# A fused attention and gated-MLP kernel: the order of VectorE's queue behind the projection, smaller pieces of the p v products, and the eviction of the first chunk

## The chip, the cores and the metric

The kernel runs on one core of a Trainium2 chip. The metric is the device time of one execution in microseconds (us). All runs told of here were with a granted TensorE clock of 1.00. Times are medians. The span of a profile (first to last instruction) is 1.7 to 1.8 us shorter than the device time of the same run. The four engines are TensorE (PE; its weight loads are PEld), VectorE (DVE), ScalarE (ACT) and GpSimd (POOL); SyncE (SP) issues the DMAs.

## The reference

Two residual blocks over x (2048 tokens, width 1024, bf16):

```python
h  = x + A(layernorm(x))       # attention, 32 heads of 32, four segments of 512 tokens;
                               # a memory M, z of phi(k) v is carried from segment to segment
h2 = h + B(layernorm(h))       # gated MLP: gelu(x @ w_in) in halves z1, z2; z2 is normalized,
                               # mixed over tokens by w_sp; (z1 * g) @ w_out
# in A, for each head and segment:
p   = softmax(q k^T * scale + mask)
o   = g * (phi(q) M) / (phi(q) z + 1e-6) + (1 - g) * (p v)
phi = lambda t: where(t > 0, t + 1, exp(t))     # the "feature map"
M, z = M + phi(k)^T v, z + sum(phi(k))
```

## The kernel before

A recording layer notes every operation in program order, and each engine executes its own in exactly that order. A wait is inserted only where the layer sees a dependency: in PSUM per bank, in SBUF per cell of 32 bytes (`GRAN`).

```python
GRAN = 32
# ...
MZB = cb("mzb", [128, NQ, 4, 34], BF16)      # 4*34*2 = 272 bytes for each of NQ = 8 groups of heads
# ...
def next_bank():                             # from n = 0 on, rot["banks"] = [6, 7]
    b = rot["banks"][rot["n"] % len(rot["banks"])]
    rot["n"] += 1
    return b

def pe_T(dst, tcl, src):                     # a 128 x 1024 chunk is transposed by TensorE, evicted by ScalarE
    b = next_bank()
    bb = bank(b).bitcast(BF16)
    for i in range(8):
        pe.transpose(bb[:, i * 128:(i + 1) * 128], src[:, i * 128:(i + 1) * 128], IDENT[:])
    act.activation(dst[:, :, tcl * 128:(tcl + 1) * 128], bb.rearrange("p (c n) -> p c n", c=8), ACTF.Copy)

def phi(n):
    # ...
    act.activation(e, q, ACTF.Exp)
    dve.tensor_single_scalar(p, q, 1.0, ALU.add)      # profile: pqk<-qk
    dve.tensor_single_scalar(e, e, 1.0, ALU.min)      # profile: etmp<-etmp
    dve.tensor_tensor(p, p, e, ALU.max)               # profile: pqk<-pqk,etmp
    # ... DMA transpose of the k half

def wo(s, tcl, half):                                 # output projection and residual
    # ...
    b = next_bank()
    mm8(bank(b), ...)                                 # profile: ps<-wo,oT
    dve.tensor_tensor(HCH[tc % 3][:, hs], XR[tc % 2][:, hs], bank(b), ALU.add)   # profile: hch<-xr,ps
    # ...

# the main loop, one round for each group of four heads and each segment
for n in range(LAST + 1):
    # ... f1, f2: K and Q products of round n + 1; f3, f4: V products or halves of wo
    split = bool(s > 0 and c > 0 and not f4)
    logits(n, 0)                              # scores, banks 0 to 3, then exp (e_104 or e_107)
    fill(f1)
    if n > 0:
        pv(n - 1, (0, 1) if split else (0, 1, 2, 3))
    logits(n, 1)                              # exp: e_105 or e_108
    if n > 0:
        state(n - 1)                          # writes msum and mzb
    bg_pop()                                  # pieces of layer norms, from a queue
    fill(f2)
    logits(n, 2)                              # exp: e_106 or e_109; mem (reads mzb), then tm by VectorE
    # ...
    if n < LAST:
        phi(n + 1)
    fill(f3)
    if split:
        pv(n - 1, (2, 3))
    bg_pop()
    fill(f4)
    bg_pop()
    # ...
```

A round asks five times for one of two banks (f1, state, f2, f3, f4). So f1 of a round takes the bank of the preceding round's f3, and f3 takes the bank that `state` used.

The softmax here doesn't subtract the row's maximum and nothing guards it: scores larger than these inputs give would overflow.

Of the kernel before, what the change touches and what calls it, by code (L numbers as in the profile page):

```python
# [5 lines left out]
BF16 = mybir.dt.bfloat16  # L6
F32 = mybir.dt.float32
I32 = mybir.dt.int32
ACTF = mybir.ActivationFunctionType
# [5 lines left out]
NSEG = 4  # L15
# [4 lines left out]
NQ = 8  # L20
# [237 lines left out]
def bass_sequential_preLN__memory_aug_infini_attn__mixer_gmlp__prompt_kernel(  # L258
# [17 lines left out]
    pe, act, dve, pool, sp = R.pe, R.act, R.dve, R.pool, R.sp  # L276
# [6 lines left out]
    def tens(name, shape, dt, off):  # L283
        sz = int(np.prod(shape[1:])) * mybir.dt.size(dt)
        assert off % 32 == 0 and off + sz <= ARENA, (name, off, sz)
        t = nc.alloc_sbuf_tensor_at(name, list(shape), dt, offset=abase + off)
        R.space[t[:].tensor.name] = ("sbuf", off)
        return t
# [14 lines left out]
    IDENT = cb("ident", [128, 128], BF16)  # L303
# [19 lines left out]
    XNT = [tens("xnT0", [128, 8, L], BF16, 30 * K), tens("xnT1", [128, 8, L], BF16, 38 * K)]  # L323
# [10 lines left out]
    XCH = [b2("xch%d" % i, [128, D], BF16) for i in range(4)]  # L334
    QK = [b2("qk%d" % i, [128, 2, L], BF16) for i in range(2)]
    PQK = [b2("pqk%d" % i, [128, 2, L], BF16) for i in range(2)]
    ETMP = b2("etmp", [128, 2, L], BF16)
# [25 lines left out]
    def bank(b):  # L363
        return PS[:, b, :]
# [6 lines left out]
    def next_bank():  # L371
# [4 lines that stand above are left out]
    def mm8(dst, lhs, rhs, n=8):  # L376
        for i in range(n):
            pe.matmul(dst, lhs(i), rhs(i), start=(i == 0), stop=(i == n - 1))
# [61 lines left out]
    def ln_apply(src, k):  # L440
        o = LNO[lno[0] % 3]
        lno[0] += 1
        dve.tensor_scalar(o[:], src[:], MV[k][:, 0:1], RS[k][:, 1:2], ALU.subtract, ALU.mult)
        return o
# [1 line left out]
    def to_T(dst, tcl, src):  # L446
        sp.dma_start_transpose(dst[:, :, tcl * 128:(tcl + 1) * 128], src[:])

    def pe_T(dst, tcl, src):
        b = next_bank()  # L450
        bb = bank(b).bitcast(BF16)
        for i in range(8):
            pe.transpose(bb[:, i * 128:(i + 1) * 128], src[:, i * 128:(i + 1) * 128], IDENT[:])
        act.activation(dst[:, :, tcl * 128:(tcl + 1) * 128], bb.rearrange("p (c n) -> p c n", c=8), ACTF.Copy)


    def proj_v(s, tcl, half):
# [2 lines left out]
    def proj_v_cols(s, tcl, lo, w):  # L460
        b = next_bank()
        xt = XNT[s % 2]
        mm8(PS[:, b, 0:w], lambda i: xt[:, i, tcl * 128:(tcl + 1) * 128], lambda i: WV[:, i, lo:lo + w])
        act.activation(V[:, tcl, lo // 32:(lo + w) // 32, 0:32],
                       PS[:, b, 0:w].rearrange("p (h d) -> p h d", d=32), ACTF.Copy)
# [6 lines left out]
        mm8(bank(b), lambda i: w[:, i, c * 128:(c + 1) * 128], lambda i: xt[:, i, :])  # L472
        act.activation(QK[n % 2][:, which, :], bank(b), ACTF.Copy)

    def phi(n):
        s, c = divmod(n, NQ)
        lo = 1 if s == 0 else 0
        hi = 1 if s == NSEG - 1 else 2
        q, p, e = QK[n % 2][:, lo:hi, :], PQK[n % 2][:, lo:hi, :], ETMP[:, lo:hi, :]
        act.activation(e, q, ACTF.Exp)  # L480
        dve.tensor_single_scalar(p, q, 1.0, ALU.add)
        dve.tensor_single_scalar(e, e, 1.0, ALU.min)
        dve.tensor_tensor(p, p, e, ALU.max)
        if s < NSEG - 1:
            sp.dma_start_transpose(PK[n % 3][:], PQK[n % 2][:, 1, :])


    def logits(n, rnd):
        qk = QK[n % 2]
        parts = {0: ((0, 0, 512),), 1: ((1, 0, 384), (3, 384, 128)), 2: ((2, 0, 256),)}[rnd]  # L490
        wid = (512, 512, 256)[rnd]
        e = E[n % 2][rnd]
        for j, o, w in parts:
            for i in range(4):
                pe.matmul(PS[:, i, o:o + w], qk[32 * i:32 * (i + 1), 1, j * 128:(j + 1) * 128],
                          qk[32 * i:32 * (i + 1), 0, j * 128:512], start=True, stop=True,
                          tile_position=(32 * i, 0))
        if rnd == 2 and n >= NQ:
            mem(n)
        act.activation(e[:, :, 0:wid], PS[:, 0:4, 0:wid], ACTF.Exp, scale=float(SCALE))  # L500
        for j, o, w in parts:
            d = e[:, :, o:o + 128]
            pool.affine_select(out=d, in_=d, pattern=[[0, 4], [1, 128]], compare_op=ALU.is_ge, fill=0.0,
                               base=0, channel_multiplier=-1)
        if rnd == 2 and n >= NQ:
            mem_norm(n)

    def pv(n, cqs):
        c = n % NQ
        for cq in cqs:  # L510
            for j in range(cq + 1):
                rnd, o = {0: (0, cq * 128), 1: (1, cq * 128 - 128), 2: (2, cq * 128 - 256), 3: (1, 384)}[j]
                for i in range(4):
                    pe.matmul(PVA[:, cq, i, :], E[n % 2][rnd][:, i, o:o + 128], V[:, j, 4 * c + i, 0:33],
                              start=(cq % 2 == 0 and j == 0 and i == 0), stop=False, skip_group_check=True)
        if 3 in cqs:
            norm(n)
# [61 lines left out]
    def ln_tasks(src, dst, tcl):  # L579
        lnq[0].append((src, dst, tcl))  # L580
# [14 lines left out]
    ks = {}  # L595

    def stats_of(tc):
        ks[tc] = ln_stats(XCH[tc])
        ln_rstd(ks[tc])


    def warm(k):
        for _ in range(k):
            pe.matmul(bank(7), IDENT[:], ETMP[:, 0, :], start=True, stop=True)

    warm(12)
    stats_of(0)
    stats_of(1)
    late = {1: [(0, 0), (0, 1)], 2: [(1, 0), (1, 1)], 3: [(2, 0), (2, 1), (3, 0), (3, 1)]}

    lns = [ln_apply(XCH[0], ks[0]), ln_apply(XCH[1], ks[1])]
    for tc in range(4):
        if tc < 2:
            stats_of(tc + 2)
        pe_T(XNT[0], tc, lns[tc])
        if tc < 2:
            warm(3)
        if tc in (1, 2):
            lns.append(ln_apply(XCH[tc + 1], ks[tc + 1]))
        for t_, q in late.get(tc, []):  # L620
            proj_v_cols(0, t_, 256 * q, 256)
    for tc in range(4, 8):
        x_load(tc)
    sp.dma_start(WK[:, :, 256:D], wcols(A_wk, 256, D))
# [1 line left out]
    gates()  # L626
    proj_qk(0, 1)
    proj_qk(0, 0)
    phi(0)
    rot["banks"] = [6, 7]  # L630

    CH = [("z2", FH + 448 * k, 448) for k in range(4)] + [("z1", 512 * k, min(512, FH - 512 * k)) for k in range(4)]
# [29 lines left out]
    LAST = NSEG * NQ - 1  # L662
    for n in range(LAST + 1):
        s, c = divmod(n, NQ)
        f1, f2, f3, f4 = [], [], [], []
        if n < LAST:
            f1, f2 = [("qk", n + 1, 1)], [("qk", n + 1, 0)]
        if s == 0:
            f3 = [("v", 0, c, 1)] if c < 4 else [("v", 1, c - 4, 0)]
        elif s < NSEG - 1:  # L670
            if c < 2:
                f3, f4 = [("v", s, 2 * c, 1)], [("v", s, 2 * c + 1, 1)]
            elif c < 6:
                f3, f4 = [("wo", s - 1, c - 2, 0)], [("wo", s - 1, c - 2, 1)]
            else:
                f3, f4 = [("v", s + 1, 2 * (c - 6), 0)], [("v", s + 1, 2 * (c - 6) + 1, 0)]
        else:
            if c < 4:
                f3 = [("v", s, c, 1)]
            if c in (2, 3):  # L680
                f4 = [("wo", s - 1, 0, c - 2)]
            elif c in (4, 5):
                f3 = [("wo", s - 1, 1, c - 4)]
            elif c == 6:
                f3, f4 = [("wo", s - 1, 2, 0)], [("wo", s - 1, 2, 1)]
            elif c == 7:
                f1, f2 = [("wo", s - 1, 3, 0)], [("wo", s - 1, 3, 1)]
                f3, f4 = [("z2", 0, 0)], [("z2", 0, 1)]

        def fill(lst):  # L690
            for u in lst:
                {"v": proj_v, "wo": wo, "qk": proj_qk, "z2": z2_group}[u[0]](*u[1:])

        if s < NSEG - 1 and c < 4:
            ln_tasks(XCH[c], XNT[(s + 1) % 2], c)
        if s < NSEG - 2 and c >= 4:
            x_load(4 * (s + 2) + c - 4)
        if s > 0 and c == 1:
            xr_load(4 * (s - 1))

        split = bool(s > 0 and c > 0 and not f4)
        logits(n, 0)
# [3 lines that stand above are left out]
        logits(n, 1)  # L706
        if n > 0:
            state(n - 1)
        bg_pop()
        fill(f2)  # L710
        logits(n, 2)
        if n == 0:
            mask_g()
        if n < LAST:
            phi(n + 1)
        fill(f3)
        if split:
            pv(n - 1, (2, 3))
        bg_pop()
        fill(f4)  # L720
        bg_pop()
        if n == 1:
            sp.dma_start(WO[:], wcols(A_wo, 0, D))
        if n in (28, 29):
            win_load(n - 28)
# [31 lines left out]
    for k in range(4, 8):  # L757
        lo, w = CH[k][1:]
        for fl in range(w // 128):
            fc = lo // 128 + fl  # L760
            for s in range(NSEG):
                b = next_bank()
# [11 lines left out]
    for tb in range(4):  # L774
# [4 lines left out]
        for fc in range(14):  # L779
            b = next_bank()  # L780
# [3 lines left out]
        for tcl in range(4):  # L784
            tc = 4 * tb + tcl
            fin = FIN[tc % 3]
            sp.dma_start(fin[:], out2d[tc * 128:(tc + 1) * 128, :])
            for lo, w in ((0, 512), (512, 512)) if tc < NTC - 1 else ((0, 512), (512, 256), (768, 256)):
                b = next_bank()
# [34 lines left out]
```

## Time and profile before

| | |
|---|---|
| time | 811.35 us (811.25 to 811.51) |
| TensorE busy, clock | 98%, 1.00 |
| a full round, from its first score product to the next round's | 9.57 us |
| the eight "late" rounds, each directly behind a projection (four from 111.21, four from 190.24 us) | 10.19 us |
| the three split rounds (from 249.08, 275.99 and 283.81 us) | 7.81, 7.82, 8.32 us |

The prediction calls the late rounds "projection rounds". The projection's products are at the end of one round and the wait for their bank is at the head of the following one; a late round is counted from the score product just ahead of that wait.

From the page of the kernel before: its span, the engines' busy times with their shares of the span and instruction counts, and one of the costliest groups (busy us, mean ns of one, then the idle time ahead of it):

```profile
span 809.5 us, 12478 instructions
...
PE 791.0 (98%) x5335; PEld 384.3 (47%) x5408; DVE 369.3 (46%) x755; ACT 302.7 (37%) x356; POOL 121.1 (15%) x234
...
L209 PE MATMUL ps<-wo,oT 128*128 128x512 bf16 x252 | 57.8, 379 | 0.3 <-DVE rd L209 0.2
```

A matmul of 512 columns takes 379 ns by its record, and there is hardly any idle time ahead of such groups. Only the stages in which TensorE waits can give something back. From the list of TensorE's waits (who waited for whom: us in total, times, longest):

```profile
PE ps L209 <- DVE hch_85 L209: 1.7, 3, 0.6
PE ps L209 <- DVE hch_86 L209: 1.6, 3, 0.6
PE ps L209 <- DVE hch_87 L209: 1.1, 2, 0.6
...
PE ps L209 <- ACT qk_96 L209: 0.7, 1, 0.7
...
PE ps L209 <- ACT e_105 L209: 0.6, 4, 0.2
PE ps L209 <- ACT e_108 L209: 0.6, 4, 0.2
```

The three hch lines are one kind of wait in three rotating buffers: 8 waits, 4.4 us. The timeline (start, us, engine, operation, in brackets the idle time ahead of it and what ended it) shows one of them:

```profile
119.61 0.69 DVE L209 TENSOR_TENSOR tm_112<-ps,rdm 128x512 f32<-128x512 f32 x1
120.22 0.42 DVE L209 TENSOR_SCALAR pqk_98<-qk_96 128x1024 bf16<-128x1024 bf16 x1
120.55 0.42 DVE L209 TENSOR_SCALAR etmp<-etmp 128x1024 bf16<-128x1024 bf16 x1
121.00 0.69 DVE L209 TENSOR_TENSOR pqk_98<-pqk_98,etmp 128x1024 bf16<-128x1024 bf16 x1
121.40 0.39 PE L209 MATMUL ps<-qk_96 32*128 32x512 bf16 x4
121.61 0.68 DVE L209 TENSOR_TENSOR hch_86<-xr_84,ps 128x512 bf16<-128x512 bf16 x1
...
122.35 1.90 PE L209 MATMUL ps<-xnT_78,wk 128*128 128x512 bf16 x8 [0.55 <-DVE hch_86 L209]
```

VectorE runs the three operations of the feature map (120.22 to 121.61) between tm and the residual addition hch. TensorE's K product needs the bank that hch empties. The feature map itself is not needed until a round later. The late round is longer than a full one by 10.19 - 9.57 = 0.62 us; the bracket says 0.55, since ends of matmuls are modelled.

One of the split rounds, at the place where the next round begins:

```profile
280.83 0.29 PE L209 MATMUL ps<-qk_96 32*128 32x256 bf16 x4 [0.15 <-ACT e_105 L209]
...
283.05 0.69 DVE L209 TENSOR_TENSOR tm_111<-ps,rdm 128x512 f32<-128x512 f32 x1
...
283.81 0.40 PE L209 MATMUL ps<-qk_97 32*128 32x512 bf16 x4
```

No wait is reported at 283.81, yet tm ends at 283.74, and the product may not start before tm has read its banks. There is no slack behind the visible absence of a wait.

The start of the kernel:

```profile
6.62 0.49 DVE L209 TENSOR_SCALAR lno_88<-xch_92,mv_63,rs_67 128x1024 bf16<-128x1024 bf16 x1
...
7.89 0.55 DVE L209 TENSOR_SCALAR lno_89<-xch_93,mv_64,rs_68 128x1024 bf16<-128x1024 bf16 x1 [0.77 <-POOL rs_68 L209]
...
21.80 0.60 ACT L209 ACTIVATE qk_96<-ps 128x512 bf16<-128x512 f32 x1 [1.13 <-PE ps L209]
...
22.45 0.39 PE L209 MATMUL ps<-qk_96 32*128 32x512 bf16 x4 [0.69 <-ACT qk_96 L209]
...
22.90 1.88 ACT L209 ACTIVATE e_104<-ps 128x2048 bf16<-128x2048 f32 x1
```

lno_88 and lno_89 are the first two normalized chunks of x. The statistics and normalizations are in one VectorE queue (GpSimd makes rs between them), and TensorE's transposes wait for them.

### The profile page before, as it was taken

How to read it: one execution, taken by the hardware profiler on the slowest of the kernel's cores; microseconds unless marked ns; L12 is line 12 of the kernel's file. 1: busy time of each engine (PE TensorE's matmuls, PEld its weight loads, DVE VectorE, ACT ScalarE, POOL GpSimd, SP SyncE). 2: the span in 40 equal slices, each digit the busy share in tenths (PEclk: the TensorE clock that was granted, in tenths of full speed). 3: DMA queues.
4: the chain of work that ended last, by engine and by line, in shares of the span. 5: the costliest groups of instructions: out<-in, count | busy, mean ns of one | idle time of the engine just before them, and what ended most of it. 6: DMA issues, size and time to landing. Idle time of an engine off the chain costs nothing.

```text
span 809.5 us, 12478 instructions
## 1 busy us (share of the span) xinstructions
PE 791.0 (98%) x5335; PEld 384.3 (47%) x5408; DVE 369.3 (46%) x755; ACT 302.7 (37%) x356; POOL 121.1 (15%) x234
## 2 busy tenths in 40 slices
PE   8999999999999999999999999999999999999998
PEld 5445544454454445455554444444444444444444
DVE  4653687668754485844463000054233324423332
ACT  4898866787678764133333333200000000000000
POOL 2343333233323331100131000000000000000000
PEclk9999999999999999999999999999999999999999
DMA  9682535355434055711114100460270044011002
GB/s 291 160 169 60 92 66 131 79 92 72 103 51 79 28 144 124 183 46 53 53 52 106 25 1 0 157 149 0 79 137 1 26 95 94 1 58 53 1 7 85
DMA packets 125992, 64.79 MB, mean 80 GB/s; under 512 B 94832, under 2 KB 114928, under 8 KB 125936
## 3 DMA queue, kind: packets, MB, share of 16 engines
q1 hardware_dynamic: 125936, 63.99, 34.4%
q8 instruction: 42, 0.69, 0.3%
q14 instruction: 14, 0.11, 0.0%
HBM read 32.51 MB, written 8.39 MB: 51 GB/s over the span
## 4 chain that ended last, share of the span: by engine, by line
PE 88%; DVE 6%; ACT 4%; issue 1%; DMA 0%; POOL 0%; DVEq 0%
PE ps L209 88%; ACT e_108 L209 1%; ACT e_105 L209 1%; DVE rdm L209 1%; DVE ta L209 1%; DVE tm_111 L209 1%; DVE stats_59 L209 0%; ACT e_106 L209 0%; DVE stats_61 L209 0%; DVE tm_112 L209 0%; DVE hch_85 L209 0%; DVE etmp L209 0%; ACT e_109 L209 0%; DMA xch_92<-in_A_x_dram 0%; DVE rd L209 0%
## 5 line engine op out<-in xcount | busy, mean ns | idle before, releaser
L209 PE MATMUL ps<-w_out,yT 128*128 128x512 bf16 (+1 forms) x453 | 96.9, 372 | 0.5
L209 PE MATMUL ps<-wspT_122,z_119 128*128 128x512 bf16 x439 | 96.5, 379 | 0.5
L209 PE MATMUL ps<-wspT_121,z_119 128*128 128x512 bf16 x439 | 96.5, 379 | 0.5
L209 PEld LDWEIGHTS ps<-w_out,yT 128*128 128x128 bf16 x462 | 45.2, 98 | 51.7
L209 PEld LDWEIGHTS ps<-wspT_121,z_119 128*128 128x128 bf16 x448 | 43.8, 98 | 52.8
L209 PEld LDWEIGHTS ps<-wspT_122,z_119 128*128 128x128 bf16 x448 | 43.8, 98 | 52.9
L209 DVE TENSOR_TENSOR tmpg_128<-ps,brow_126 128x512 f32<-128x512 f32 x14 | 9.7, 691 | 116.9 <-DMA brow_126<-in_B_b_sp_dram 96.6
L209 ACT ACTIVATE z_119<-ps 128x448 bf16<-128x448 f32 x64 | 34.8, 544 | 75.1 <-PE ps L209 74.9
L209 PE MATMUL ps<-wo,oT 128*128 128x512 bf16 x252 | 57.8, 379 | 0.3 <-DVE rd L209 0.2
L209 ACT ACTIVATE z1T<-ps 128x512 bf16<-128x512 f32 x56 | 33.4, 597 | 63.3 <-PE ps L209 63.3
L209 DVE BATCH_NORM_STATS2 zst<-z_119 128x6 f32<-128x448 bf16 x64 | 39.2, 620 | 33.2 <-ACT z_119 L209 33.2
L209 PEld LDWEIGHTS ps<-wo,oT 128*128 128x128 bf16 x256 | 24.4, 98 | 27.5 <-DVE hch_86 L209 0.3
L209 ACT ACTIVATE e_107<-ps 128x2048 bf16<-128x2048 f32 x16 | 30.0, 1874 | 12.7 <-PE ps L209 12.7
L209 ACT ACTIVATE e_108<-ps 128x2048 bf16<-128x2048 f32 x16 | 30.0, 1878 | 10.8 <-PE ps L209 10.8
L209 ACT ACTIVATE e_104<-ps 128x2048 bf16<-128x2048 f32 x16 | 30.0, 1876 | 10.4 <-PE ps L209 10.4
L209 ACT ACTIVATE e_105<-ps 128x2048 bf16<-128x2048 f32 x16 | 30.0, 1877 | 9.8 <-PE ps L209 9.8
L209 PE MATMUL ps<-xnT_78,wk 128*128 128x512 bf16 x126 | 29.9, 380 | 2.5 <-DVE hch_85 L209 1.1
L209 PE MATMUL ps<-xnT_77,wk 128*128 128x512 bf16 x127 | 30.2, 380 | 2.3 <-DVE hch_86 L209 1.1
L209 PE MATMUL ps<-wv,xnT_78 128*128 128x512 bf16 x128 | 29.6, 379 | 0.0
L209 PE MATMUL ps<-wv,xnT_77 128*128 128x512 bf16 (+1 forms) x159 | 29.5, 336 | 0.1
L209 PE MATMUL ps<-xnT_78,wq 128*128 128x512 bf16 x113 | 27.0, 379 | 1.3 <-issue 0.6
L209 PE MATMUL ps<-xnT_77,wq 128*128 128x512 bf16 x114 | 27.2, 379 | 0.7
(217 smaller groups left out, 1169.6 us busy)
## 6 DMA issues: line engine op xcount, KB each, us to landing
w_out<-in_B_w_out_dram SPq DMA_DIRECT2D x1, 3584.0 KB, 12.7
wo<-in_A_wo_dram SPq DMA_DIRECT2D x1, 2048.0 KB, 10.6
xr_83<-in_A_x_dram SPq DMA_DIRECT2D x8, 256.0 KB, 3.1
xr_84<-in_A_x_dram SPq DMA_DIRECT2D x8, 256.0 KB, 3.0
win_116<-in_B_w_in_dram SPq DMA_DIRECT2D x2, 896.0 KB, 4.9
wk<-in_A_wk_dram SPq DMA_DIRECT2D x1, 1536.0 KB, 11.4
wq<-in_A_wq_dram SPq DMA_DIRECT2D x1, 1536.0 KB, 15.0
out_dram<-hch_85 SPq DMA_DIRECT2D x6, 256.0 KB, 3.0
```

The source lines that it names most:

```text
L209: ins = getattr(e, op.name)(*op.args, **op.kw)
```

## The change

The intent is to take waits out of TensorE's queue. The change has three independent parts. Part 1 moves VectorE's share of the feature map behind f3, so the residual addition goes ahead of it. Part 2 moves the products of p with v (`pv`) for the third token quarter, in the split rounds (those in which f4 is empty), ahead of the third score product. Part 3 evicts the first chunk by ScalarE and VectorE from two banks, and reorders the first V, K and Q products (normalized x with a weight) so that the last V products fill the wait for qk_96.

```diff
-    def pe_T(dst, tcl, src):
-        b = next_bank()
-        ...
+    def pe_T(dst, tcl, src, engines=(act,)):
+        w = 8 // len(engines)
+        for k, eng in enumerate(engines):
+            bb = bank(next_bank()).bitcast(BF16)[:, 0:w * 128]
+            ...                                   # w transposes
+            if eng is act:
+                act.activation(d, v, ACTF.Copy)
+            else:
+                dve.tensor_copy(d, v)
@@
-    def phi(n):
+    def phi_exp(n):
+        q, p, e = phi_views(n)
         act.activation(e, q, ACTF.Exp)
+
+    def phi_max(n):
+        q, p, e = phi_views(n)
         dve.tensor_single_scalar(p, q, 1.0, ALU.add)
         dve.tensor_single_scalar(e, e, 1.0, ALU.min)
         dve.tensor_tensor(p, p, e, ALU.max)
         ...
@@ start: order of the first products
-    # T0 warm(3) | T1 warm(3) V0 | T2 V1 | T3 V2 V3 | K Q | phi(0)
+    # T0 (act, dve) warm(3) | T1 warm(2) V0 | T2 V1 | T3 V2 | K Q V3 | phi_exp(0) phi_max(0)
     ...
@@ main loop
         fill(f2)
+        if split:
+            pv(n - 1, (2,))
         logits(n, 2)
         ...
         if n < LAST:
-            phi(n + 1)
+            phi_exp(n + 1)
         fill(f3)
+        if n < LAST:
+            phi_max(n + 1)
         if split:
-            pv(n - 1, (2, 3))
+            pv(n - 1, (3,))
```

(The start is shown as two comment lines: T is a chunk's transposes, V its two quarter V products; warm(k) is k products whose results nobody reads.)

More of the change, by code (lines that the diff above doesn't have):

```diff
@@ L447, in to_T @@
         sp.dma_start_transpose(dst[:, :, tcl * 128:(tcl + 1) * 128], src[:])
-    def pe_T(dst, tcl, src):
-        b = next_bank()
-        bb = bank(b).bitcast(BF16)
-        for i in range(8):
-            pe.transpose(bb[:, i * 128:(i + 1) * 128], src[:, i * 128:(i + 1) * 128], IDENT[:])
-        act.activation(dst[:, :, tcl * 128:(tcl + 1) * 128], bb.rearrange("p (c n) -> p c n", c=8), ACTF.Copy)
+    def pe_T(dst, tcl, src, engines=(act,)):
+        w = 8 // len(engines)
+        for k, eng in enumerate(engines):
+            bb = bank(next_bank()).bitcast(BF16)[:, 0:w * 128]
+            for i in range(w):
+                o = (k * w + i) * 128
+                pe.transpose(bb[:, i * 128:(i + 1) * 128], src[:, o:o + 128], IDENT[:])
+            d = dst[:, k * w:(k + 1) * w, tcl * 128:(tcl + 1) * 128]
+            v = bb.rearrange("p (c n) -> p c n", c=w)
+            if eng is act:
+                act.activation(d, v, ACTF.Copy)
+            else:
+                dve.tensor_copy(d, v)
     def proj_v(s, tcl, half):
@@ L473, in proj_qk, with phi_views @@
         act.activation(QK[n % 2][:, which, :], bank(b), ACTF.Copy)
-    def phi(n):
-        s, c = divmod(n, NQ)
+    def phi_views(n):
+        s = n // NQ
         lo = 1 if s == 0 else 0
         hi = 1 if s == NSEG - 1 else 2
-        q, p, e = QK[n % 2][:, lo:hi, :], PQK[n % 2][:, lo:hi, :], ETMP[:, lo:hi, :]
+        return QK[n % 2][:, lo:hi, :], PQK[n % 2][:, lo:hi, :], ETMP[:, lo:hi, :]
+    def phi_exp(n):
+        q, p, e = phi_views(n)
         act.activation(e, q, ACTF.Exp)
+    def phi_max(n):
+        q, p, e = phi_views(n)
         dve.tensor_single_scalar(p, q, 1.0, ALU.add)
@@ L483, in phi @@
         dve.tensor_tensor(p, p, e, ALU.max)
-        if s < NSEG - 1:
+        if n // NQ < NSEG - 1:
             sp.dma_start_transpose(PK[n % 3][:], PQK[n % 2][:, 1, :])
@@ L604, in warm, with v_quarter @@
             pe.matmul(bank(7), IDENT[:], ETMP[:, 0, :], start=True, stop=True)
+    def v_quarter(tcl, q):
+        proj_v_cols(0, tcl, 256 * q, 256)
     warm(12)
@@ L608, in bass_sequential_preLN__memory_aug_infini_attn__mixer_gmlp__prompt_kernel @@
     stats_of(1)
-    late = {1: [(0, 0), (0, 1)], 2: [(1, 0), (1, 1)], 3: [(2, 0), (2, 1), (3, 0), (3, 1)]}
-    lns = [ln_apply(XCH[0], ks[0]), ln_apply(XCH[1], ks[1])]
-    for tc in range(4):
-        if tc < 2:
-            stats_of(tc + 2)
-        pe_T(XNT[0], tc, lns[tc])
-        if tc < 2:
-            warm(3)
-        if tc in (1, 2):
-            lns.append(ln_apply(XCH[tc + 1], ks[tc + 1]))
-        for t_, q in late.get(tc, []):
-            proj_v_cols(0, t_, 256 * q, 256)
+    ln0 = ln_apply(XCH[0], ks[0])
+    pe_T(XNT[0], 0, ln0, (act, dve))
+    warm(3)
+    ln1 = ln_apply(XCH[1], ks[1])
+    stats_of(2)
+    pe_T(XNT[0], 1, ln1)
+    warm(2)
+    stats_of(3)
+    v_quarter(0, 0)
+    v_quarter(0, 1)
+    ln2 = ln_apply(XCH[2], ks[2])
+    ln3 = ln_apply(XCH[3], ks[3])
+    pe_T(XNT[0], 2, ln2)
+    v_quarter(1, 0)
+    v_quarter(1, 1)
+    pe_T(XNT[0], 3, ln3)
+    v_quarter(2, 0)
+    v_quarter(2, 1)
     for tc in range(4, 8):
@@ L628, in bass_sequential_preLN__memory_aug_infini_attn__mixer_gmlp__prompt_kernel @@
     proj_qk(0, 0)
-    phi(0)
+    v_quarter(3, 0)
+    v_quarter(3, 1)
+    phi_exp(0)
+    phi_max(0)
     rot["banks"] = [6, 7]
```

## The prediction

> **What bounds the kernel now.** TensorE: the page gives it 791.0 of 809.5 us busy (98%), clock 1.00. The chain of waits is TensorE alone from 329 us on. TensorE's timeline gives the round period: 9.57 us in a full round, but 10.19 us in the eight that compute the output projection (four from 111.2, four from 190.2 us). In each of these TensorE idles 0.55 us before the next K product, released by "hch", VectorE's residual addition that empties the bank (list of waits: 8 waits, 4.4 us). The chain shows tm, then pqk, etmp, pqk (the feature map, about 1.35 us), then hch (0.69 us).
>
> **Part 1, residual ahead of the feature map.** hch can start when tm ends (120.3 us in the round from 111.2) and end near 121.0; TensorE needs the bank about 121.75. The wait should vanish. Gross: 8 x 0.62 = 5.0 us. Deduction: with two layer norms in flight VectorE has about 9.8 us of work in the second such round of each group (0.36 us idle in 10.19), more than 9.57. Its lag should reach "msum" a round later, which frees that projection's bank: I expect a new 0.3 us wait in the third projection round of each group, then slack (VectorE idles 1.56 us there). Net 4.4 us. The round at 292 us: perhaps 0.1.
>
> **Part 2, V products in three parts.** Only three rounds split (from 249, 276 and 284 us). The moved part, 12 products, about 0.30 us, fits the 0.3 us in which TensorE waits for e_105/e_108. But the next round's first product needs e_106/e_109 and then tm, which ends 0.07 us before that product starts already (283.74, 283.81; 292.05, 292.13; 256.82, 256.89). The freed 0.3 us becomes a wait for tm. Worth 0 (-0.1 to +0.2).
>
> **Part 3, first chunk by two engines.** ScalarE's 1.02 us eviction is halved, but TensorE's next transposes wait for lno_89, not for it, and VectorE's new copy stands ahead of lno_89. Estimate: a 512-element PSUM operation takes 0.69 us at one element a cycle; the Trainium skill ("VectorE: DVE Perf Modes", "Why PSUM operands drop a tier") caps a PSUM source at 2x_1P, so about 0.42 us for bf16; no run shows this copy yet. It delays lno_89 (7.89) by 0.3 to 0.5 us, and the chain to lno_90 (11.46) slides along. In return the last V products fill the 0.69 us in which TensorE waited for qk_96, but what follows is a ScalarE chain (qk_96, etmp, e_104): its exp now waits for a 0.38 us V eviction instead of a 0.60 us one. Net: e_104 (22.90 now) starts 0.05 to 0.3 us later; about 0.15 us lost.
>
> **Sum.** 811.35 - 4.4 - 0.1 + 0.15 = 807.0 us, range 806.0 to 808.3. Faster by over 2% 1%, within 98%, slower 1%.
>
> **What would show each step.** Right: no TensorE waits on hch in projection rounds; period 9.6 us, one per group near 9.9 with a wait on msum; from 250 to 300 us unchanged periods (7.81, 7.82, 8.32) and waits on tm in place of e_105/e_108; lno_89 at 8.2 to 8.4, e_104 at 23.0 to 23.2. Wrong: hch waits that only shrink; split rounds 0.2 us shorter; e_104 before 22.8.
>
> **What would make it wrong.** No msum wait (806.5); VectorE's lag reaching tm or hch too (808); a residual load, whose order against the transposes changes, landing late; a copy over 0.7 us; part 2 gaining 0.3 us a round (806).

## The result and the profile after

| | before | after |
|---|---|---|
| time, median | 811.36 us (6 runs) | 806.94 us (6 runs, 806.82 to 807.40) |
| ratio | | 0.9946, 95% interval 0.9933 to 0.9959 |
| late rounds, first group | 10.19, 10.19, 10.19, 10.19 | 9.70, 9.57, 9.68, 9.57 |
| late rounds, second group | 10.18, 10.19, 10.20, 10.18 | 9.69, 9.57, 9.69, 9.56 |
| split rounds | 7.81, 7.82, 8.32 | 7.88, 7.87, 8.39 |

A ratio is the mean time of one kernel's fast runs over that of the other's of the same rounds, so it is not quite the ratio of the medians quoted beside it.

The same two lines of the changed kernel's page, then its list of TensorE's waits:

```profile
span 805.2 us, 12550 instructions
...
PE 796.1 (99%) x5407; PEld 384.7 (48%) x5407; DVE 368.7 (46%) x756; ACT 301.8 (37%) x356; POOL 121.5 (15%) x234
```

```profile
PE ps L209 <- DVE tm_111 L209: 0.8, 2, 0.6
...
PE ps L209 <- ACT e_104 L209: 0.6, 1, 0.6
PE ps L209 <- ACT e_105 L209: 0.5, 3, 0.2
PE ps L209 <- DVE tm_112 L209: 0.4, 2, 0.2
...
PE ps L209 <- ACT e_108 L209: 0.3, 2, 0.2
```

No hch line is left. The tm lines have grown: before, there was one tm wait of 0.6 us in all. The timeline of the round that answers to the one shown of before:

```profile
119.01 0.69 DVE L209 TENSOR_TENSOR tm_112<-ps,rdm 128x512 f32<-128x512 f32 x1
119.62 0.68 DVE L209 TENSOR_TENSOR hch_86<-xr_84,ps 128x512 bf16<-128x512 bf16 x1
120.21 0.42 DVE L209 TENSOR_SCALAR pqk_98<-qk_96 128x1024 bf16<-128x1024 bf16 x1
120.55 0.42 DVE L209 TENSOR_SCALAR etmp<-etmp 128x1024 bf16<-128x1024 bf16 x1
120.81 0.40 PE L209 MATMUL ps<-qk_96 32*128 32x512 bf16 x4
121.00 0.69 DVE L209 TENSOR_TENSOR pqk_98<-pqk_98,etmp 128x1024 bf16<-128x1024 bf16 x1
121.13 1.90 PE L209 MATMUL ps<-xnT_78,wk 128*128 128x512 bf16 x8
```

hch ends at 120.30 and the K product starts at 121.13 without a wait, with 0.8 us to spare. The two groups together are shorter by (40.76 - 38.52) + (40.75 - 38.51) = 4.48 us, nearly the whole gain. But two late rounds of each group are 9.69 us instead of 9.57. In the first of them:

```profile
116.65 0.30 DVE L209 TENSOR_TENSOR mzb<-msum,maskg 128x132 bf16<-128x132 f32 x1
116.67 0.29 PE L209 MATMUL ps<-qk_97 32*128 32x256 bf16 x4
117.00 0.23 PEld L209 LDWEIGHTS ps<-mzb,pqk_99 128*128 128x128 bf16 x4 [0.24 <-DVE mzb L209]
117.01 0.41 PE L209 MATMUL ps<-mzb,pqk_99 128*128 128x132 bf16 x4
```

The weight load for the product with mzb waits for VectorE's write of mzb. The distance between these two products is 117.01 - 116.67 = 0.34 us, where rounds without the wait have 0.22.

The split round of before, now:

```profile
276.39 0.29 PE L209 MATMUL ps<-qk_96 32*128 32x256 bf16 x4
...
279.36 0.40 PE L209 MATMUL ps<-qk_97 32*128 32x512 bf16 x4 [0.22 <-DVE tm_111 L209]
```

The wait ahead of the third score product is gone and a wait for tm stands at the head of the next round. The round has become longer.

The start:

```profile
6.55 0.50 DVE L209 TENSOR_SCALAR lno_88<-xch_92,mv_63,rs_67 128x1024 bf16<-128x1024 bf16 x1
...
7.76 0.42 DVE L209 COPY xnT_77<-ps 128x512 bf16<-128x512 bf16 x1 [0.71 <-PE ps L209]
8.11 0.54 DVE L209 TENSOR_SCALAR lno_89<-xch_93,mv_64,rs_68 128x1024 bf16<-128x1024 bf16 x1
...
21.91 0.39 PE L209 MATMUL ps<-qk_96 32*128 32x512 bf16 x4
...
22.81 1.87 ACT L209 ACTIVATE e_104<-ps 128x2048 bf16<-128x2048 f32 x1
```

TensorE's first score product is 0.54 us earlier, but the exp that follows, e_104, is only 0.09 us earlier, of which 0.07 is there already at lno_88: this run's first x chunk had landed earlier. Measured from lno_88, e_104 starts after 16.26 us here and after 16.28 us before. So the start gained 0.02 us: ahead of e_104 ScalarE's queue still holds the eviction of a V product (0.38 us from 22.01) and etmp (from 22.29).

### The profile page after: what moved, and what is told of

Same layout as the page of the kernel before. It is cut to its first block, busy times and chain, and to the rows that moved or that the text cites. A ratio compares the mean times of both kernels' runs of the same rounds, so it can differ in the third digit from the quotient of the medians.

```text
span 805.2 us, 12550 instructions
## 1 busy us (share of the span) xinstructions
PE 796.1 (99%) x5407; PEld 384.7 (48%) x5407; DVE 368.7 (46%) x756; ACT 301.8 (37%) x356; POOL 121.5 (15%) x234
## 3 DMA queue, kind: packets, MB, share of 16 engines
HBM read 32.51 MB, written 8.39 MB: 51 GB/s over the span
## 4 chain that ended last, share of the span: by engine, by line
PE 92%; DVE 5%; ACT 2%; issue 1%; DMA 0%
PE ps L209 92%; ACT e_105 L209 1%; DVE ta L209 1%; DVE stats_61 L209 0%; DVE stats_62 L209 0%; ACT e_108 L209 0%; DVE rdm L209 0%; DMA xch_92<-in_A_x_dram 0%; DVE hch_85 L209 0%; DVE rd L209 0%; ACT e_109 L209 0%; ACT e_106 L209 0%; DVE pqk_99 L209 0%; ACT e_104 L209 0%; DVE stats_59 L209 0%
## 5 line engine op out<-in xcount | busy, mean ns | idle before, releaser
L209 PE MATMUL ps<-xnT_78,wq 128*128 128x512 bf16 x128 | 30.3, 379 | 0.0
L209 PE MATMUL ps<-xnT_77,wq 128*128 128x512 bf16 x128 | 30.2, 379 | 0.0
```

Source lines behind the costliest of these rows:

```text
L209: ins = getattr(e, op.name)(*op.args, **op.kw)
```

## The experiments

All eleven kernels gave correct results, and each was timed in 5 rounds against the kernel before, whose median was 811.32 to 811.34 us. In these profiles the names carry no buffer numbers (hch for hch_85).

| run | time, us | ratio to before, 95% interval | late rounds, first group | e_104 behind the first lno, us |
|---|---|---|---|---|
| p1_only | 806.75 | 0.9943 (0.9931, 0.9956) | 9.69 9.56 9.69 9.57 | 16.28 |
| p2_only | 811.50 | 1.0002 (0.9989, 1.0015) | 10.18 10.19 10.20 10.18 | 16.28 |
| p3_only | 811.38 | 1.0000 (0.9988, 1.0013) | 10.19 10.18 10.20 10.18 | 16.26 |
| p1_p3 | 806.82 | 0.9945 (0.9931, 0.9958) | 9.69 9.57 9.68 9.57 | 16.26 |
| after_pad | 806.55 | 0.9941 (0.9929, 0.9954) | 9.56 9.58 9.58 9.57 | 16.26 |
| p1_max | 806.09 | 0.9936 (0.9922, 0.9950) | 9.57 9.56 9.58 9.57 | 16.28 |
| p1_halfmax | 809.30 | 0.9975 (0.9962, 0.9987) | 9.92 9.92 9.93 9.92 | 16.27 |
| reorder_act | 806.51 | 0.9941 (0.9928, 0.9953) | 9.68 9.58 9.67 9.57 | 15.98 |
| p1_add | 806.76 | 0.9944 (0.9932, 0.9956) | 9.69 9.57 9.68 9.57 | 16.28 |
| max_reorder | 805.88 | 0.9933 (0.9920, 0.9945) | 9.57 9.57 9.58 9.56 | 15.98 |
| max_reorder_pad | 805.71 | 0.9933 (0.9920, 0.9947) | 9.57 9.56 9.58 9.57 | 15.99 |

The intervals of the ratios are wider than some of the differences that matter here (0.1 to 0.3 us are 0.01% to 0.04%), so for these the round periods in the profiles decide, and times are only asked whether they agree.

### p1_only: part 1 alone

```diff
-            phi(n + 1)
+            phi_exp(n + 1)
         fill(f3)
+        if n < LAST:
+            phi_max(n + 1)
```

> Part 1 alone (residual addition ahead of the feature map), all else as before. Theory A (the parts add, part 1 carries nearly all): the eight projection rounds fall from 10.19 us to alternating 9.70 and 9.57, 2 x 2.24 = 4.5 us in all, so 806.9 us. The split rounds keep 7.81, 7.82 and 8.32 us and the first exp of scores (e_104) starts at 22.9 us as before. Rival B (the gain needs the freer start or the V products in three parts as well): less than 3.5 us gained, above 807.9 us.

Measured: 806.75 us, 4.58 us below before. The late rounds, the split rounds (7.82, 7.81, 8.33) and e_104 are as theory A had them. Part 1 carries the whole gain; rival B is out.

### p2_only: part 2 alone

```diff
         fill(f2)
+        if split:
+            pv(n - 1, (2,))
         logits(n, 2)
...
-            pv(n - 1, (2, 3))
+            pv(n - 1, (3,))
```

> Part 2 alone (V products of three split rounds in three parts). Theory A: the wait of TensorE before the third score product only moves to a wait for tm at the next round's first product, and since the 12 moved products do not quite fit the gap, each of the three split rounds becomes 0.07 us longer: 7.88, 7.87 to 7.89 and 8.39 us, total 811.55 us. Rival C (part 2 gains alone and was only spoilt by the other parts, for example by the residual that now stands ahead of the feature map): split rounds shorter than 7.81, 7.82 and 8.32 us, total at most 811.2 us.

Measured: 811.50 us and split rounds of 7.88, 7.87 and 8.40 us, against 7.81, 7.82 and 8.32. In the list of TensorE's waits tm has 4 entries and 1.3 us, where before had one of 0.6. Rival C is out: part 2 loses about 0.06 us in each of three rounds, also without the other parts. The ratio alone would not have shown it.

### p3_only: part 3 alone

```diff
-    def pe_T(dst, tcl, src):
+    def pe_T(dst, tcl, src, engines=(act,)):      # as in the change
...
-    # T0 warm(3) | T1 warm(3) V0 | T2 V1 | T3 V2 V3 | K Q | phi(0)
+    # T0 (act, dve) warm(3) | T1 warm(2) V0 | T2 V1 | T3 V2 | K Q V3 | phi(0)
```

> Part 3 alone (start of the kernel). Theory A: lno_89 starts 0.2 us later because VectorE's copy of 0.42 us stands ahead of it, but e_104 starts about 0.1 us earlier (22.8 against 22.9 us), so 811.25 us; all rounds from 29 us on as before. Rival D (the earlier e_104 in the changed kernel came from an x chunk that happened to land 0.07 us earlier): e_104 at 22.9 us or later when measured from the first statistics instruction, no gain, 811.35 us or more.

Measured: 811.38 us, no gain. lno_89 starts 1.55 us behind the first lno instead of 1.27, and e_104 starts 16.26 us behind it instead of 16.28. My expectation of 811.25 us was a miss and rival D was right: most of the 0.09 us seen in the changed kernel's profile came from when the first chunk landed. In the thirteen profiles the first lno starts between 6.47 and 6.71 us, so an absolute time at the start says little without that anchor.

### p1_p3: the changed kernel without part 2

```diff
         fill(f2)
-        if split:
-            pv(n - 1, (2,))
         logits(n, 2)
...
-            pv(n - 1, (3,))
+            pv(n - 1, (2, 3))
```

> The changed kernel with part 2 undone. Theory A (part 2 costs 3 x 0.07 us): 806.7 us, 0.2 us below the changed kernel, split rounds back at 7.81, 7.82 and 8.32 us, projection rounds unchanged. Rival C (part 2 is neutral or gains): 806.95 us or more.

Measured: 806.82 us, between the two forecasts; the times leave it open. The split rounds are back at 7.82, 7.82 and 8.32 us, and that confirms p2_only from the other side.

### reorder_act: new order at the start, old eviction

```diff
-    pe_T(XNT[0], 0, ln0, (act, dve))
+    pe_T(XNT[0], 0, ln0)
```

This is against p1_p3.

> The changed kernel without part 2, and with the first chunk's transposes evicted by ScalarE alone in one bank as before; the new order of the first V, K and Q products stays. Theory A (VectorE's copy only delays lno_89, the gain at the start is all from the new order): lno_89 starts 0.2 us earlier than in the changed kernel, e_104 about 0.2 us earlier (22.6 us), total 806.5 us. Rival I (the eviction by two engines is what gains, since the first V products can start sooner): e_104 at 22.9 us or later, total 806.9 us or more.

Measured: 806.51 us; the second lno is again 1.26 us behind the first (1.56 in p1_p3), and e_104 comes 15.98 us behind the first lno, 0.28 us earlier than with both engines. Theory A holds: the new order gains 0.30 us at the start, and VectorE's copy gives 0.28 us of it back. (The new order also has one warm product less. That is not what gained: the transposes of the last chunk start 7.59 us behind the first lno before and 7.58 us here, so the gain arises later, where the last V products are moved behind K and Q.)

### p1_halfmax and p1_max: how much must be deferred

Both are against part 1 alone. In p1_max only the last operation of the feature map goes behind the residual addition. In p1_halfmax only half of that operation does.

```diff
     def phi_exp(n):
         act.activation(e, q, ACTF.Exp)
+        dve.tensor_single_scalar(p, q, 1.0, ALU.add)
+        dve.tensor_single_scalar(e, e, 1.0, ALU.min)
+        # p1_halfmax only:
+        dve.tensor_tensor(p[:, :, 0:256], p[:, :, 0:256], e[:, :, 0:256], ALU.max)
     def phi_max(n):
-        dve.tensor_single_scalar(p, q, 1.0, ALU.add)
-        dve.tensor_single_scalar(e, e, 1.0, ALU.min)
-        dve.tensor_tensor(p, p, e, ALU.max)
+        dve.tensor_tensor(p, p, e, ALU.max)     # p1_halfmax: columns 256 to 511
```

> As before, but only half of the max (256 of the 512 columns of each of the two rows) goes behind the residual addition; the other half stays ahead of it, and one instruction is added to each feature map. Theory A: the residual addition starts about 0.26 us earlier than before (1.13 instead of 1.39 us behind tm), so the wait on hch shrinks from 0.55 to about 0.3 us; projection rounds 9.93 us, total 809.3 us. Rival H (the order of the queue alone matters, not the time at which the bank is free): no gain, 811.3 us, or the whole gain.

> As part 1 alone, but only the last of the feature map's three VectorE operations (the max, 0.61 us from start to start) goes behind the residual addition; the other two stay ahead of it. Theory A (what counts is only that the bank is free by the time TensorE asks for it, 0.55 us earlier than before): the wait on hch disappears just as with all three deferred, projection rounds 9.57 to 9.75 us, total 806.9 us plus or minus 0.3. Rival G (the gain grows with the work that is deferred): 0.61 of 1.39 us deferred gives 44% of the gain, 809.4 us.

Measured for p1_halfmax: 809.30 us, late rounds of 9.92 us, as theory A had said, and the wait has shrunk to half. From its list of TensorE's waits:

```profile
PE ps L209 <- DVE hch L209: 2.3, 8, 0.3
```

Rival H is out: the wait follows the time at which the bank is free. Measured for p1_max: 806.09 us and no wait on hch. Rival G (809.4 us) is out; once the bank is free in time, a longer deferral brings nothing. But p1_max is also 0.66 us faster than p1_only, where theory A allowed no more than 0.3 us beyond 806.9. All its late rounds are 9.57 us; the stalls of 0.12 us are gone although mzb is as it was. Its VectorE queue shows the difference:

```profile
118.83 0.69 DVE L209 TENSOR_TENSOR tm<-ps,rdm 128x512 f32<-128x512 f32 x1
119.44 0.42 DVE L209 TENSOR_SCALAR pqk<-qk 128x1024 bf16<-128x1024 bf16 x1
119.78 0.42 DVE L209 TENSOR_SCALAR etmp<-etmp 128x1024 bf16<-128x1024 bf16 x1
120.11 0.68 DVE L209 TENSOR_TENSOR hch<-xr,ps 128x512 bf16<-128x512 bf16 x1
120.71 0.68 DVE L209 TENSOR_TENSOR pqk<-pqk,etmp 128x1024 bf16<-128x1024 bf16 x1
```

From the start of the min (etmp) to the next operation it is 0.33 us here, but 0.45 us in the changed kernel (120.55 to 121.00), where the max comes next and needs the min's result.

### p1_add: is it the neighbours?

Against part 1 alone, too. Here the residual addition stands between add and min, so min and max are neighbours again.

```diff
     def phi_exp(n):
         act.activation(e, q, ACTF.Exp)
+        dve.tensor_single_scalar(p, q, 1.0, ALU.add)
     def phi_max(n):
-        dve.tensor_single_scalar(p, q, 1.0, ALU.add)
         dve.tensor_single_scalar(e, e, 1.0, ALU.min)
         dve.tensor_tensor(p, p, e, ALU.max)
```

> The residual addition stands between the feature map's add and its min; min and max both come behind it. Deferring only the max gave 806.1 us, less than deferring all three (806.75), with every projection round at 9.57 us. Theory J: that extra came from VectorE's min and max no longer standing next to each other: the max waits for the min's result, so min to max takes 0.45 us from start to start, but min to residual addition 0.33, and the 0.12 us saved keep mzb from being late. Here min and max are neighbours again, so the stalls in the first and third projection round of each group return (9.69 us) and the total is 806.75 us. Rival K (what counts is how early the feature map is done): this kernel lies between the two, rounds below 9.65 us, total 806.2 to 806.5 us.

Measured: 806.76 us, late rounds of 9.69, 9.57, 9.68 and 9.57 us, split rounds of 7.82, 7.82 and 8.32 us. Theory J's numbers were met, and those of rival K (806.2 to 806.5 us) were not. The 0.12 us that a dependent neighbour costs decides; to bring only the add forward gains nothing. The run does not fully test rival K, though: the feature map's last operation, the max, starts 1.99 us behind tm here as in p1_only, and 1.88 us behind it in p1_max, so the map is finished no earlier than in p1_only. p1_max also has shorter rounds at 8.20 and 9.91 us where p1_only has 8.33 and 10.03; there TensorE waits for ta, which is behind the same VectorE operations (waits for ta 0.4 instead of 0.6 us in all).

### after_pad: the wait on mzb

```diff
-    MZB = cb("mzb", [128, NQ, 4, 34], BF16)
+    MZB = cb("mzb", [128, NQ, 4, 36], BF16)      # 288 bytes, a multiple of 32
```

A group's block of mzb has 272 bytes, 8.5 cells of 32. Block 3 begins in the cell in which block 2 ends, so the product that reads block 3 is made to wait for the write of block 2, which the round's `state` makes. This happens for odd blocks only, and the stalls are in every second late round.

> The changed kernel with each block of mzb padded from 272 to 288 bytes, nothing else. In the changed kernel TensorE loses 0.12 us in the first and third projection round of each group, ahead of the product with mzb, which the list of dependencies makes wait for VectorE's write of the neighbouring block, because the two blocks share one 32-byte cell of the kernel's own dependency tracking. Theory E (that false dependency is the wait): these four rounds fall from 9.69 to 9.57 us, unless the next wait in line, the one on msum, takes part of it back in the round after; total 0.3 to 0.5 us below the changed kernel, 806.5 us. Rival F (the loss is VectorE's load in general and would be taken by whatever waits next): rounds stay at 9.69 us or the loss moves to their neighbours, total 806.9 us.

Measured: 806.55 us, 0.39 us below the changed kernel, with late rounds of 9.56 to 9.58 us. In the place shown above it now reads:

```profile
116.72 0.30 DVE L209 TENSOR_TENSOR mzb<-msum,maskg 128x132 bf16<-128x132 f32 x1
116.74 0.29 PE L209 MATMUL ps<-qk 32*128 32x256 bf16 x4
...
116.96 0.41 PE L209 MATMUL ps<-mzb,pqk 128*128 128x132 bf16 x4
```

The product starts while the write of the neighbouring block is still under way. Theory E holds; the dependency was false. The loss did not move on to msum either: in the following round msum ends at 126.71 and the projection that needs its bank starts at 126.77, just in time.

### max_reorder and max_reorder_pad: the best pieces together

Against reorder_act, which has no part 2 (the second kernel also has the padding):

```diff
     def phi_exp(n):
         act.activation(e, q, ACTF.Exp)
+        dve.tensor_single_scalar(p, q, 1.0, ALU.add)
+        dve.tensor_single_scalar(e, e, 1.0, ALU.min)
     def phi_max(n):
-        dve.tensor_single_scalar(p, q, 1.0, ALU.add)
-        dve.tensor_single_scalar(e, e, 1.0, ALU.min)
         dve.tensor_tensor(p, p, e, ALU.max)
```

> The best pieces together: only the max behind the residual addition, the changed kernel's new order of the first V, K and Q products with the first chunk evicted by ScalarE alone, and no part 2. If the gains add: 806.1 (max alone) less 0.3 us for the start (e_104 at 16.0 us behind the first normalized chunk's start, against 16.28 before), 805.8 us, all projection rounds 9.57 us. If they do not add: 806.1 us or more.

> The same with the blocks of mzb padded to 288 bytes. Theory E with J: with only the max deferred mzb is already written before TensorE asks, so the padding has nothing left to remove: 805.8 us, within 0.1 us of the kernel without padding, rounds 9.57 us in both. Rival: the padding gains again (0.3 us or more, 805.5 us), so the stall that it removes was not the one that deferring the max removes.

Measured: 805.88 and 805.71 us. The gains add. Both beat the kernel before and the changed kernel (by 1.06 and 1.23 us by the medians). The padding's difference of 0.17 us is more than the 0.1 us that I allowed, but the rounds of the two are the same to 0.01 us and the second's first lno came 0.10 us earlier (6.58 against 6.68 us), so the profiles show no stall that the padding removed. Nor do the times settle it: one run of the padded kernel took 806.38 us, and the means of the five are 805.86 with and 805.85 us without the padding.

## Why the prediction was right or wrong

The time was right: 807.0 us predicted, 806.94 measured. That it is so close is in part luck, because errors of the terms cancel: the late rounds gave 0.08 us more than the 4.4 us forecast and the start 0.17 us more, but the split rounds lost 0.19 us where nothing was forecast, and the round at 292 us, "perhaps 0.1", gained nothing (10.04 us before, 10.06 after).

- **Part 1, the bound and the gain: right.** The eight waits on hch vanished, with 0.8 us to spare. The net gain predicted was 4.4 us; the rounds of the changed kernel show 4.48 and p1_only's time 4.58. p1_halfmax shows that the waits end when the bank is free, and p1_max that nothing more is gained beyond that.
- **The deduction for VectorE's load: the size was nearly right, the step was wrong.** The failed step is "I expect a new 0.3 us wait in the third projection round of each group", on msum. VectorE's lag was there, but TensorE met it at the product with mzb, in the first late round of each group as well as in the third, the one named: 2 x 0.12 us in each group instead of 0.3. after_pad shows that this wait came from a false dependency in the kernel's own tracking, p1_max and p1_add that 0.12 us of VectorE time decide whether it is met. msum was never late: in the changed kernel's first group it ends 0.06 us before TensorE needs its bank in the second late round (126.76, 126.82) and 0.64 us before in the third (135.87, 136.51). The deduction came out right in sum (0.24 us a group against 0.3) for another reason than the one given.
- **Part 2: the mechanism right, the size a little off.** Predicted was "The freed 0.3 us becomes a wait for tm. Worth 0". The waits changed places as predicted. The mis-sized term is that the twelve products, "about 0.30 us", fit the gap: in the changed round shown they put 0.39 us between their start and the third score product (276.00 to 276.39). That product is about 0.07 us later (2.45 us behind the second one, 2.38 before), tm too, and three rounds lose 0.07, 0.05 and 0.07 us.
- **Part 3: the two opposed terms right in sign, their sum off.** The copy took 0.42 us, as estimated from the Trainium skill ("VectorE: DVE Perf Modes", "Why PSUM operands drop a tier"), and delayed lno_89 by 0.28 us from the first lno (predicted 0.3 to 0.5). The mis-sized term is the gain of the new order: about 0.2 us implied (by its own 0.60 less 0.38 us), 0.30 measured by reorder_act. So a loss of 0.15 us became none: e_104 came at 22.81, not "at 23.0 to 23.2".

## What to carry to other kernels

In a queue that executes in order, put the operation that frees a contended buffer ahead of work that nobody awaits; only as much need be moved as makes the buffer free in time. Then use such an operation as the separator between two that depend on each other, because an independent neighbour hides the wait that a dependent one pays (0.33 against 0.45 us from start to start here). When a wait for an engine appears at a place where the data have no reason for it, look for two neighbours that share a unit of the dependency tracking, and before a gap is filled, look at what the next wait in line is bound by.

## What the Trainium skill lacked or had wrong

- "VectorE: DVE Perf Modes", section "The DRAIN you can't avoid": it reports that in a chain of copies a semaphore after each "costs nothing extra". That does not carry over to these runs: a max that waits for the preceding min's result starts 0.45 us behind the min's start, but an addition that does not wait for VectorE starts 0.33 us behind it; these 0.12 us decided whether TensorE stalled for 0.12 us in the first and third late rounds (p1_max against p1_add). The same section's remark that a next operation that isn't held starts earlier agrees with the trace: hch starts 0.61 us behind tm, whose record lasts 0.69 us.
- "VectorE: DVE Perf Modes", section "Why PSUM operands drop a tier", has nothing to put right: its cap of twice the rate for a 16-bit PSUM source agrees with the copy of 512 elements, 0.42 us, against 0.69 us for a 512-element addition from PSUM.
- No page that I looked up tells how far the landing of a kernel's first load moves from run to run: the first normalization started between 6.47 and 6.71 us in thirteen profiles, more than several of the effects studied here.
